# Linear attention with a gated MLP on one core: query and key features in groups of 128, 128, 128, 128, 64 rows, with the last group's low parts stacked under its high parts

## The chip, the cores and the metric

The kernel runs on one core of a Trainium2 chip. The metric is device time in microseconds (us), here of that one core. The engines are TensorE (PE; its weight loads are PEld), VectorE (DVE), ScalarE (ACT), GpSimd (POOL) and SyncE (SP, which issues most DMAs). Each works through its own queue in order; semaphores tie the queues together.

## What is computed

With x of 2048 tokens and 576 features, the kernel mixes two branches by a gate per token. The reference, cut to what matters:

```python
g = sigmoid((x * gate_w).sum(-1, keepdims=True))
# branch A, 32 heads of 18 features
q, k, v = split(x @ wqkv)
phi = lambda t: where(t > 0, t + 1, exp(t)) + 1e-6
pq, pk = phi(q), phi(k)
kv = einsum("bhsd,bhse->bhde", pk, v)          # per head
z = einsum("bhsd->bhd", pk)
num = einsum("bhqd,bhde->bhqe", pq, kv)
den = einsum("bhqd,bhd->bhq", pq, z)[..., None] + 1e-6
a = (num / den) @ wo
# branch B, Df = 4608
b = (gelu(x @ w_gate) * (x @ w_up)) @ w_down
return g * a + (1 - g) * b
```

## The kernel before

**Precision by parts.** Every fp32 operand is split into a rounded high part and a low part (the rest). ScalarE makes the high part, VectorE or GpSimd the low part (`split`, L67 to L69). A product is then three matmuls: high by high, high by low, low by high. They add up in the same PSUM bank.

**Stages.** (1) To about 119 us: key projections and, per 128 tokens, x^T times the key features (`grams`, L235), so that no value projection over tokens is needed. (2) To about 283 us: "mixing", the stage that the change edits. (3) The gate and up products of the MLP (L830), by a seven-product scheme, to about 1100 us, and (4) the down products (L1093) to the end. The first chain of stage 3 is interleaved with the end of stage 2.

**Heads in groups.** The 576 features of keys and queries lie in five groups of 7, 7, 7, 7 and 4 heads, that is 126, 126, 126, 126 and 72 rows (`GH`, `GR`, `GO`, L19 to L21). A group g fills one set of partitions.

**Mixing.** The order is written out by hand as a list of calls (L468 to L810, `tc.manual_schedule()`): what stands first in the text stands first in each engine's queue. Blocks b of 512 tokens come in the order 2, 3, 0, 1. The calls are:

- `query(b, g)` (L426): 14 matmuls of 512 tokens (L433) into one of three PSUM banks; then ScalarE's Relu (L435) and Exp (L436), and VectorE's L437, which gives r. L437 is the last reader of the bank.
- `states(kt)` (L445): kv per group from the grams and the value weights, ten matmuls for each of five kt (L452, L454); `key_sums_mm` (L462) the sums z.
- `states_out` (L523) and `key_sums` (L538) turn both into SBUF operands: kvt with a mask by heads, and zmk, whose columns pick the heads (L542, L543).
- `head_out(g)` (L546): a group's kv times its rows of wo (L553), split into KW[g]. `wo_load(g)` (L515) loads those rows and splits them (L519, L520); the loads stand in SP's queue.
- `halves_of(b, g)` (L561): r + eps as high part (ScalarE, L565) and low part (VectorE, L566), the tile hl, of which there are two. `den(b, g)` (L569): two matmuls (L575) that add the group's part to the denominators of all heads.
- `reciprocal(b, h)` (L640): denominators of 256 tokens to SBUF (L644, L645), reciprocal (L646), store to DRAM (L647). `reciprocals_load` (L649) reads them back (L651), each head's row repeated on its 18 partitions.
- `scaled(b, t)` (L670) for 128 tokens: r times the reciprocal (VectorE, L663), then the split into p, high part on ScalarE (L68) and low part on VectorE (L69).
- `mixed(b, t)` (L674): 5 groups x 3 parts x 2 column halves, 30 matmuls of 288 columns (L682) into one of two PSUM pairs; ScalarE scales the result by the gate (L687) and issues its store itself (L689).

Around the change the list interleaves these by hand: for example query(0,4) stands behind `reciprocals(3)` and ahead of scaled(2,2), and query(1,4) behind halves_of(1,0) and (1,1) and ahead of mixed(3,2). Token sums (L287 to L290 on VectorE, L621 on ScalarE) and loads for stage 3 are put between them. Behind query(1,4) ScalarE loads the table for Gelu (L772).

## Time and profile before

| | |
|---|---|
| time, median of 3 runs | 1504.03 us (1503.03 to 1504.7) |
| the profiled execution | 1503.88 us |
| its span, first to last instruction | 1502.1 us |
| mean granted TensorE clock | 1.000 |
| matmul queries, L433 | 280 matmuls, 14 for each of 20 (b, g) |
| matmul mixing, L682 | 480 matmuls, 30 for each of 16 (b, t) |
| matmul denominators, L575 | 40 matmuls |
| HBM read, written | 156.72 MB, 88.24 MB |

The page gives the busy time of each engine and its share of the span; matmuls are pipelined, so a busy PE is not PE at its peak, and the time from one matmul's start to the next tells more than the duration of one. The chain of waits goes back from the last instruction, at each step to what released it or to the one before it on its engine. A timeline row has its start, its duration (of a merged row, from the first start to the last end), the operation with out<-in, and in brackets how long the engine was idle before and for whom. All starts are in us from the span's start.

### The profile page before, as it was taken

How to read it: one execution, taken by the hardware profiler on the slowest of the kernel's cores; microseconds unless marked ns; L12 is line 12 of the kernel's file. 1: busy time of each engine (PE TensorE's matmuls, PEld its weight loads, DVE VectorE, ACT ScalarE, POOL GpSimd, SP SyncE). 2: the span in 40 equal slices, each digit the busy share in tenths (PEclk: the TensorE clock that was granted, in tenths of full speed). 3: DMA queues.
4: the chain of work that ended last, by engine and by line, in shares of the span. 5: the costliest groups of instructions: out<-in, count | busy, mean ns of one | idle time of the engine just before them, and what ended most of it. 6: DMA issues, size and time to landing. Idle time of an engine off the chain costs nothing.

```text
span 1502.1 us, 21595 instructions
## 1 busy us (share of the span) xinstructions
PE 1495.4 (100%) x8354; PEld 1320.4 (88%) x8354; DVE 1000.8 (67%) x1324; ACT 546.5 (36%) x711; POOL 716.6 (48%) x516
## 2 busy tenths in 40 slices
PE   9999999999999999999999999999999999999999
PEld 9998889878888888888888888888899999999999
DVE  7887776574666555666556665556677677777775
ACT  7554645333222233222232222332234454444431
POOL 1674533246554554654644644544347354553710
PEclk9999999999999999999999999999999999999999
DMA  7563464662333222332223332224777646565564
GB/s 250 166 205 118 165 249 166 240 248 91 141 140 115 96 106 105 140 141 97 100 102 123 141 122 103 99 98 167 292 285 265 213 153 216 169 213 187 198 201 136
DMA packets 98638, 246.36 MB, mean 164 GB/s; under 512 B 9056, under 2 KB 36344, under 8 KB 96104
## 3 DMA queue, kind: packets, MB, share of 16 engines
q1 hardware_dynamic: 95656, 235.42, 45.3%
q10 hardware_dynamic: 2880, 9.57, 1.8%
q8 instruction: 65, 1.06, 0.3%
q14 instruction: 37, 0.30, 0.1%
HBM read 156.72 MB, written 88.24 MB: 163 GB/s over the span
## 4 chain that ended last, share of the span: by engine, by line
PE 94%; DVE 3%; ACT 1%; issue 1%; DMA 1%; SPq 0%; ACTq 0%; DVEq 0%
PE bank L830 53%; PE bank L1093 27%; PE bank L433 4%; PE pair L682 3%; PE pair L244 2%; PE pair L199 2%; PE kpair L244 2%; PE kpair L199 2%; DMA raw<-wk 1%; DVE e L855 0%; PE den L575 0%; ACT p L68 0%; DVE r L663 0%; DVE hl L566 0%; PE pair L553 0%
## 5 line engine op out<-in xcount | busy, mean ns | idle before, releaser
L830 PE MATMUL bank<-xo,wg 128*128 128x512 f32 x1764 | 414.0, 395 | 1.3 <-DVE e L862 0.8
L830 PE MATMUL bank<-xo,wu 128*128 128x512 f32 (+1 forms) x1715 | 402.0, 395 | 0.1
L830 PEld LDWEIGHTS bank<-xo,wg 128*128 128x128 f32 x1764 | 332.2, 189 | 79.2 <-DVE e L862 1.2
L830 PEld LDWEIGHTS bank<-xo,wu 128*128 128x128 f32 (+1 forms) x1715 | 323.2, 189 | 75.8 <-ACT p L871 0.5
L1101 DVE SCALAR_TENSOR_TENSOR acc<-bank,gate,acc 128x288 f32<-128x288 f32 x288 | 140.7, 513 | 71.2 <-PE bank L1093 69.4
L283 POOL TENSOR_TENSOR stage<-stage 128x384 f32<-128x384 f32 x132 | 153.5, 1183 | 51.0 <-DMA stage<-wgu 48.4
L871 ACT ACTIVATE p<-bank 128x512 f32<-128x512 f32 x72 | 43.1, 599 | 332.4 <-PE bank L830 332.0
L844 POOL TENSOR_TENSOR wg<-stage,wg 128x768 fp32r<-128x768 f32 (+1 forms) x34 | 72.9, 2145 | 177.0 <-ACT wg L843 175.7
L844 POOL TENSOR_TENSOR wu<-stage,wu 128x768 fp32r<-128x768 f32 (+1 forms) x34 | 79.9, 2351 | 149.0 <-ACT wu L843 147.8
L1093 PE MATMUL bank<-wd,xo 128*128 128x288 f32 x1008 | 135.8, 294 | 0.0
L1093 PEld LDWEIGHTS bank<-wd,xo 128*128 128x128 f32 x1008 | 134.1, 188 | 0.0
L979 POOL TENSOR_TENSOR xo<-stage,xo 128x432 fp32r<-128x432 f32 x44 | 65.4, 1509 | 113.2 <-ACT xo L977 113.2
L876 DVE TENSOR_TENSOR u<-bank,p 128x512 f32<-128x512 f32 x72 | 49.5, 687 | 96.3 <-PE bank L830 86.8
L1093 PE MATMUL bank<-xo 128*128 128x288 f32 x792 | 107.1, 295 | 0.1
L1093 PEld LDWEIGHTS bank<-xo 128*128 128x128 f32 x792 | 105.7, 188 | 0.5 <-DVE u L865 0.4
L979 POOL TENSOR_TENSOR wd<-stage,wd 128x432 fp32r<-128x432 f32 x40 | 59.4, 1510 | 90.9 <-ACT wd L977 90.9
L862 DVE TENSOR_TENSOR e<-bank,u 128x512 f32<-128x512 f32 x54 | 37.2, 691 | 77.0 <-PE bank L830 76.9
L862 DVE TENSOR_TENSOR f<-bank,u 128x512 f32<-128x512 f32 x54 | 37.3, 692 | 71.6 <-PE bank L830 71.3
L852 ACT ACTIVATE f<-f 128x512 f32<-128x512 f32 x54 | 34.1, 633 | 132.8 <-DVE f L862 132.7
L984 POOL TENSOR_TENSOR stage<-stage 128x432 f32<-128x432 f32 x48 | 75.8, 1605 | 0.0
L890 DVE TENSOR_TENSOR u<-bank,u 128x512 f32<-128x512 f32 x72 | 49.8, 692 | 35.5 <-PE bank L830 33.3
L682 PEld LDWEIGHTS pair<-kw,p 126*128 126x128 f32 (+1 forms) x480 | 65.0, 188 | 2.0 <-DVE p L69 0.6
(192 smaller groups left out, 2310.0 us busy)
## 6 DMA issues: line engine op xcount, KB each, us to landing
h_d<-sx SPq DMA_DIRECT2D x108, 256.0 KB
stage<-wgu SPq DMA_DIRECT2D x34, 768.0 KB
xo<-h_d SPq DMA_DIRECT2D x29, 768.0 KB
e<-h_d SPq DMA_DIRECT2D x28, 768.0 KB
hraw<-h_d SPq DMA_DIRECT2D x27, 768.0 KB
h_d<-e SPq DMA_DIRECT2D x72, 256.0 KB
h_d<-f SPq DMA_DIRECT2D x72, 256.0 KB
stage<-wdn SPq DMA_DIRECT2D x6, 1728.0 KB
```

The source lines that it names most:

```text
L199: nc.tensor.matmul(out_t[:, :n], xa, kvw[i][:rows, r, lo:lo + n], start=(k == 0), stop=(k == 13))
L244: nc.tensor.matmul(y[:, n, :KH], a, p[:, n * KH:(n + 1) * KH], start=(k == 0), stop=(k == len(ops) - 1))
L283: nc.gpsimd.tensor_tensor(o, a, b, OP.subtract)
L433: nc.tensor.matmul(ps[:R], qw[i][:rows, rw, GO[g]:GO[g] + R], xa, start=(k == 0), stop=(k == 13))
L682: nc.tensor.matmul(y[:, i, :288], p[:R, a, g], KW[g][:R, wl, i * 288:(i + 1) * 288], start=(n == 0), stop=(n == 14))
L830: nc.tensor.matmul(ps, w_, x_, start=start and i == 0, stop=i == 6, skip_group_check=not start)
L844: nc.gpsimd.tensor_tensor(w[:, i, 3:5], src[:, :, 0:2], f32(w[:, i, 0:2]), OP.subtract)
L862: nc.vector.tensor_tensor(es[i], a, b, OP.add)
L979: nc.gpsimd.tensor_tensor(w[:, 1, c], src[:, c], f32(w[:, 0, c]), OP.subtract)
L984: nc.gpsimd.tensor_tensor(draw[:, o, c], draw[:, x, c], draw[:, y, c], OP.subtract)
L1093: nc.tensor.matmul(y, h[:, hl, g, t * 128:(t + 1) * 128], w[:, wl, g * 288:(g + 1) * 288], start=k in (1, 5) and n == 0, stop=n == len(ops ...
L1101: nc.vector.scalar_tensor_tensor(o, y, gate[:, 1, st:st + 1], o, op0=OP.mult, op1=OP.add)
```

## The change

Groups of query and key features now have 128, 128, 128, 128 and 64 rows: the 64 features that don't fit a fifth full group fill the two free partitions of each of the first four (`QORDER` gives the feature at each place). The value side and wo keep the old groups of 126 and 72 (`VR`, `VO`). What follows:

- **queries**: the fifth group's weights lie as 64 high columns and, right behind them, 64 low columns, so that one matmul of 128 columns gives both products with the high part of x. It has ten matmuls instead of 14. The lower products come out on partitions 64 to 127 and are added to the upper ones: a ScalarE copy, then a VectorE add within PSUM, both ahead of Relu.
- **halves_of, den**: for the fifth group the low part is written to partitions 64 to 127 of the same column block, and one matmul with a doubled zmk takes the place of two. `key_sums` makes zmk's second half with two more operations.
- **scaled_parts, mixed**: the fifth group's p has its low part under its high part, and KW[4] is repeated below itself (`rows_again`); two parts instead of three, 28 matmuls instead of 30. The low part is now made by two VectorE operations instead of one.
- **states**: two more small matmuls for each kt, for the key features that lie in other groups than their values.
- **head groups** in the order 4, 0, 1, 2, 3. `rows_out` copies the eight moved rows of KW[4] to the partitions 126 and 127 of KW[0] to KW[3] by four DMAs in SP's queue.
- **reciprocals**: 40 rows instead of 35; the read-back has a second DMA for the partitions 126 and 127.
- the query weights' low parts are made by two VectorE operations instead of one (`q_part`).

On VectorE, from the second block's reciprocals to the token sums, the queue reads before (L437 is the end of query(0,4), L663 and L69 are scaled(2,2)):

```order
L646 RECIPROCAL rb<-rb 35x256
L437 SCALAR_TENSOR_TENSOR r<-bank,r 72x512
L663 SCALAR_TENSOR_TENSOR r<-r,rb 126x5x128
L69 TENSOR_TENSOR p<-r,p 126x640
L287 TENSOR_TENSOR xc<-xc 128x512
```

and now:

```order
L690 RECIPROCAL rb<-rb 40x256
L459 TENSOR_TENSOR bank<-bank,r 64x512
L462 SCALAR_TENSOR_TENSOR r<-bank,r 64x512
L709 SCALAR_TENSOR_TENSOR r<-r,rb 128x5x128
L715 TENSOR_TENSOR p<-r,p 128x512
L716 TENSOR_TENSOR p<-r,p 64x128
L300 TENSOR_TENSOR xc<-xc 128x512
```

The add L459 stands between the reciprocal and the old next step, and the low part is two operations. On ScalarE the same place reads before (L644 reads the denominators, L435 and L436 are Relu and Exp of query(0,4), L68 the high part p(2,2)):

```order
L644 ACTIVATE rb<-den 35x256 x2
L435 ACTIVATE r<-bank 72x512
L436 ACTIVATE r<-r 72x512
L68 ACTIVATE p<-r 126x640
L687 ACTIVATE ga<-pair,gate 128x576
```

and now:

```order
L688 ACTIVATE rb<-den 40x256 x2
L458 ACTIVATE r<-bank 64x512
L460 ACTIVATE r<-bank 64x512
L461 ACTIVATE r<-r 64x512
L714 ACTIVATE p<-r 128x640
L734 ACTIVATE ga<-pair,gate 128x576
```

L458 is the copy that the add needs, and L460 is Relu, which needs the add. In SP's queue, the loads of wo's rows (raw<-wo) before:

```order
L302 DMA xsum_d_74<-xu 128x1024
L296 DMA xu<-xs 128x4x256
L517 DMA raw<-wo 128x576
L296 DMA xu<-xs 128x4x256
L517 DMA raw<-wo 128x576
L302 DMA xsum_d_75<-xu 128x1024
```

and now, with the four copies of KW rows:

```order
L315 DMA xsum_d_74<-xu 128x1024
L309 DMA xu<-xs 128x4x256
L593 DMA kw_1883<-kw_1887 2x1152
L593 DMA kw_1884<-kw_1887 2x1152
L593 DMA kw_1885<-kw_1887 2x1152
L593 DMA kw_1886<-kw_1887 2x1152
L549 DMA raw<-wo 128x576
L309 DMA xu<-xs 128x4x256
L549 DMA raw<-wo 128x576
```

Two loads of wo and what is behind them now follow four DMAs that read KW[4]. The diff, cut to its core:

```diff
-GH = [7, 7, 7, 7, 4]
-GR = [n * DH for n in GH]
-GO = [126 * g for g in range(5)]
+VR, VO = [126, 126, 126, 126, 72], [126 * g for g in range(5)]
+QR, QO = [128, 128, 128, 128, 64], [128 * g for g in range(5)]
+QORDER = [d for g in range(4) for d in (*range(126 * g, 126 * g + 126), 568 + 2 * g, 569 + 2 * g)] + [*range(504, 568)]
...
+    def q_part(w, kt, raw):
...
+            nc.scalar.activation(w[:, h:h + D], raw, AF.Copy)
+            nc.vector.tensor_tensor(w[:, l:l + 512], raw[:, :512], f32(w[:, h:h + 512]), OP.subtract)
+            nc.vector.tensor_tensor(w[:, h + D:h + 640], raw[:, 512:], f32(w[:, h + 512:h + D]), OP.subtract)
...
     def query(b, g):
-        R = GR[g]
+        R = QR[g]
...
+        for k, (wa, xa) in enumerate(ops):
+            nc.tensor.matmul(ps[:wa.shape[1]], wa, xa, start=(k == 0), stop=(k == len(ops) - 1), skip_group_check=g == 4)
+        if g == 4:
+            nc.scalar.activation(r, ps[64:], AF.Copy)
+            nc.vector.tensor_tensor(ps[:R], ps[:R], r, OP.add)
         nc.scalar.activation(r, ps[:R], AF.Relu, scale=-1.0)
...
     def states(kt):
...
+            parts = [(o[:, :, :n], o[:, 0, :n], gm[:, :, c])]
+            if g == 4:
+                more = gm[:, :, :512].rearrange("p a (g c) -> p a g c", g=4)[:, :, :, 126:]
+                into = o[:, :, 64:].rearrange("p a (g c) -> p a g c", g=4)
+                parts.append((into, into[:, 0], more))
...
     def states_out():
...
+        split(kvt[:72, 0, 4, :72], kvt[:72, 1, 4, :72], kvm[:72, 4, :72])
         split(kvt[:126, 0, :4], kvt[:126, 1, :4], kvm[:126, :4])
-        split(kvt[:72, 0, 4, :72], kvt[:72, 1, 4, :72], kvm[:72, 4, :72])
...
     def key_sums():
...
+            for rows in (slice(0, R),) if g < 4 else (slice(0, 64), slice(64, 128)):
+                nc.vector.tensor_scalar(zmk[rows, g, :64], sg, z, None, op0=OP.mult)
+                nc.vector.scalar_tensor_tensor(zmk[rows, g, 64:], sg, z, f32(zmk[:R, g, :64]),
+                                               op0=OP.mult, op1=OP.subtract)
...
+    def rows_out():
+        for g in range(4):
+            nc.sync.dma_start(f32(KW[g][126:]), f32(KW[4][64 + 2 * g:66 + 2 * g]))
+
+    def rows_again():
+        nc.scalar.activation(KW[4][64:, 0], f32(KW[4][:64, 0]), AF.Copy)
...
     def halves_of(b, g):
...
+        lo = hl[:, 1] if g < 4 else hl[64:, 0]
         nc.scalar.activation(hl[:R, 0], r, AF.Copy, bias=EPS)
-        nc.vector.scalar_tensor_tensor(hl[:R, 1], r, EPS, f32(hl[:R, 0]), op0=OP.add, op1=OP.subtract)
+        nc.vector.scalar_tensor_tensor(lo, r, EPS, f32(hl[:R, 0]), op0=OP.add, op1=OP.subtract)
...
-        for a in range(2):
-            nc.tensor.matmul(den_of[b], zmk[:GR[g], g], hl[:GR[g], a], start=(g == 0 and a == 0),
-                             stop=(g == NG - 1 and a == 1), skip_group_check=True)
+        for a in range(2 if g < 4 else 1):
+            nc.tensor.matmul(den_of[b], zmk[:, g], hl[:, a], start=(g == 0 and a == 0),
+                             stop=g == NG - 1, skip_group_check=True)
...
+    WO = (4, 0, 1, 2, 3)
...
-        head_out(g)
+        head_out(WO[g])
+        if g == 1:
+            rows_out()
         if g + 2 < NG:
-            wo_load(g + 2)
+            wo_load(WO[g + 2])
...
+        for k, (rows, heads, times) in enumerate(((slice(0, 126), 7, DH), (slice(126, 128), 1, 2))):
+            nc.sync.dma_start(rb_of[b, h][rows], bass.AP(
...
     def scaled_parts(b, t):
...
-        split(p[:126, 0], p[:126, 1], r)
+        nc.scalar.activation(p[:, 0], r, AF.Copy)
+        nc.vector.tensor_tensor(p[:, 1, :4], r[:, :4], f32(p[:, 0, :4]), OP.subtract)
+        nc.vector.tensor_tensor(p[64:, 0, 4], r[:64, 4], f32(p[:64, 0, 4]), OP.subtract)
...
-            for a, wl in ((0, 0), (0, 1), (1, 0)):
+            for a, wl, R in ((0, 0, 128), (0, 1, QR[g]), (1, 0, 128))[:3 if g < 4 else 2]:
...
     halves_of(3, 1)
+    rows_again()
```

More of the change, by code (lines that the diff above doesn't have):

```diff
@@ L47, in tile_gated_mix @@
     probe = keep.tile([128, 8], F32, name="probe")
-    rden_d = {(b, h): dram.tile([7 * NG, BS // 2], F32, name=f"rden_d{b}{h}") for b in range(NB) for h in range(2)}
+    rden_d = {(b, h): dram.tile([HROWS * NG, BS // 2], F32, name=f"rden_d{b}{h}") for b in range(NB) for h in range(2)}
     xop_d = dram.tile([128, 3, 5, BS], F32, name="xop_d")
@@ L100, in tile_gated_mix @@
     x8 = qwp.tile([128, 5, BS], F32R, name="x8")
-    qw = [qwp.tile([128, 5, D], F32R, name=f"qw{i}") for i in range(2)]
+    qw = [qwp.tile([128, 5 * D], F32R, name=f"qw{i}") for i in range(2)]
+    Q_HI, Q_LO = (0, 640, 1280), (1856, 2368)
     aheads = Scope()
@@ L268, in load @@
             nc.sync.dma_start(raw[:, :D], wq[i, kt])
-            todo.append(lambda: w_part(qw[i], kt, raw, 0, D))
+            todo.append(lambda: q_part(qw[i], kt, raw[:, :D]))
         else:
```

86 lines of the change are left out of this document (50 added, 36 removed).

## The prediction

> **What bounds the kernel now.** I read the page first, then the busy time by stretch, then the chain of waits in order of time, then each engine's timeline from 119 to 311 us, the only stretch in which edited instructions matter. The page:
>
> ```profile
> span 1502.1 us, 21595 instructions
> PE 1495.4 (100%) x8354; PEld 1320.4 (88%) x8354; DVE 1000.8 (67%) x1324; ACT 546.5 (36%) x711; POOL 716.6 (48%) x516
> ```
>
> TensorE is busy all the time, so the first reading is that every matmul taken out is time won. The stretches (length, then PE, PEld, DVE, ACT, POOL busy, clock, DMA share, GB/s) say that this holds in the mixing part too:
>
> ```profile
> 119.30:191.15 71.85, 71.85 (x395) 60.85 (x394) 49.60 (x80) 38.35 (x69) 29.98 (x26) 1.00 0.42 150
> 191.15:243.35 52.20, 52.14 (x316) 46.03 (x314) 37.47 (x47) 29.03 (x44) 19.58 (x20) 1.00 0.57 205
> 243.35:283.00 39.65, 39.58 (x270) 37.79 (x271) 19.75 (x25) 15.28 (x21) 6.82 (x4) 1.00 0.73 254
> ```
>
> The chain of waits (start, us, engine, tile, line) tells more:
>
> ```profile
> 171.30 0.46 PE den L575 x2
> ...
> 191.15 3.25 PE bank L433 x14
> 194.40 4.00 PE pair L682 x30
> ...
> 209.62 0.73 ACT ga L687
> ...
> 235.27 0.49 ACT r L435
> ...
> 236.44 0.53 ACT L772
> ...
> 242.47 0.84 DVE p L69
> 243.35 3.71 PE pair L682 x26
> ...
> 310.02 786.47 PE bank L830 x3381
> ```
>
> From 209.62 to 243.35 no piece of the chain is TensorE's: ScalarE and VectorE hand work to each other in program order without a pause, and at 243.35 mixed(0,0) waits for the low part p. The timeline of VectorE shows that this tight run starts earlier, right behind mixed(2,0), which ends at 191.15:
>
> ```profile
> 192.76 0.41 DVE L645 TENSOR_TENSOR rb<-rb,den 35x256 f32<-35x256 f32 x1 [1.80 <-ACT rb L644]
> ...
> 195.27 1.75 DVE L646 RECIPROCAL rb<-rb 35x256 f32<-35x256 f32 x1
> 196.94 0.62 DVE L437 SCALAR_TENSOR_TENSOR r<-bank,r 72x512 f32<-72x512 f32 x1
> ...
> 199.09 0.83 DVE L69 TENSOR_TENSOR p<-r,p 126x640 fp32r<-126x640 f32 x1 [0.81 <-ACT p L68]
> 199.84 0.95 DVE L287 TENSOR_TENSOR xc<-xc 128x512 f32<-128x512 f32 x1
> ```
>
> Followed from 191.15 (copy out of mixed(2,0), two reciprocals, query(0,4), scale(2,2), and so on), no step up to 243.35 waits for TensorE. So this stretch has two bounds of the same length, 52.2 us of matmuls and 52.2 us of ScalarE and VectorE in turn. The change shortens the first and lengthens the second. From 310.02 on TensorE alone counts, and nothing there is edited.
>
> **The change: TensorE's own work.** A query matmul takes 3.25/14 = 0.232 us, a denominator 0.46/2 = 0.23, one of mixing 4.00/30 = 0.133. Removed: 4 x 4 query matmuls 3.71, 4 denominators 0.92, 16 x 2 of mixing 4.27, together 8.9. Added: two narrow state matmuls for each of five kt. The nearest rows are the last group's pair and what follows it:
>
> ```profile
> 144.75 0.24 PE L452 MATMUL bank<-gt,wv 128*72 128x144 f32 x1
> 144.83 0.20 PE L454 MATMUL bank<-gt,wv 128*72 128x72 f32 x1
> 144.87 1.14 PE L465 MATMUL bank<-ones,rs 128*126 128x2 f32 x10
> ```
>
> Two starts in 0.12 us: 0.06 each; the ten of one stationary load with 2 columns take about 0.1 each, so 0.6 to 1.0 for ten, of which I take 0.6, the row with the same 72 weight columns. The net is -8.3 us. Whether it is kept is decided stretch by stretch.
>
> **Up to 119 us.** The query weights' low parts become two pieces (four more VectorE operations), in a part where TensorE leads, and the last one is read only behind the others: 0.
>
> **119 to 191 us.** query(b,4) gets a ScalarE copy of the upper half and a VectorE add, and Relu and Exp now stand behind that add; ScalarE takes nothing else meanwhile. The rows around query(2,4), ScalarE, VectorE and TensorE:
>
> ```profile
> 150.30 0.58 ACT L435 ACTIVATE r<-bank 72x512 f32<-72x512 f32 x1
> 150.91 0.63 ACT L436 ACTIVATE r<-r 72x512 f32<-72x512 f32 x1
> ```
> ```profile
> 152.96 0.24 DVE L542 TENSOR_SCALAR zmk<-cs,zc 72x64 fp32r<-72x64 f32 x1
> ...
> 153.44 0.68 DVE L437 SCALAR_TENSOR_TENSOR r<-bank,r 72x512 f32<-72x512 f32 x1
> ...
> 177.62 0.62 DVE L566 SCALAR_TENSOR_TENSOR hl<-r,hl 126x512 fp32r<-126x512 f32 x1
> ```
> ```profile
> 156.39 0.63 PE L575 MATMUL den<-hl,zmk 126*128 126x512 f32 x2
> ...
> 178.08 1.07 PE L575 MATMUL den<-hl,zmk 126*128 126x512 f32 x4
> ```
>
> Today Relu and Exp of query(2,4) are done while VectorE still makes zmk. Now the add stands behind a sixth pair of zmk operations (153.44 - 152.96 = 0.48) and states that end about 0.48 later: at 154.40. Add 0.68, Relu 0.58, Exp 0.63 and three or four hand-overs of 0.03 to 0.04: L437 at 156.42, the low part hl(2,0) done at 157.7. TensorE gets to den(2,0) at 156.39 + 0.60 - 0.93 = 156.06 and to its second matmul at 156.3: a wait of 1.45. Likewise hl(3,1) stands on VectorE behind query(3,4), four KW low parts and two reciprocals: 178.24 done today, about 1.3 later now (copy 0.58, add 0.68), against den(3,1) at about 178.75: a wait of 0.8. mixed(2,0) waits some 0.25 more for p(2,0). Sum: +0.6, two queries -1.86, two denominators -0.46, one tile -0.27, waits +2.5: **+0.5** when mixed(2,0) ends. Reversing the order of the head groups costs nothing itself: the same loads, copies and matmuls in another order.
>
> SP's queue: its four copies of KW rows wait for KW[4], and two loads of wo that are issued at about 143 today stand behind them.
>
> ```profile
> 143.61 0.57 SPq L517 DMA_DIRECT2D raw<-wo  x1
> ...
> 253.54 0.27 SPq L647 DMA_DIRECT2D rden_d<-rb  x1
> 255.00 0.76 SPq L651 DMA_DIRECT2D rb<-rden_d  x1
> ...
> 277.08 0.33 SPq L834 DMA_DIRECT2D stage<-wgu  x1
> ```
> ```profile
> 283.22 4.07 POOL L283 TENSOR_TENSOR stage<-stage 128x384 f32<-128x384 f32 x4 [23.50 <-DMA stage<-wgu]
> ```
>
> KW[4] is split at about 161 (behind L437 at 156.42 ScalarE has two hl copies, four Relu and Exp of 0.6 and the split itself); four issues of some 0.35 and the load's own make 163. A small write is back 1.2 us after its issue (253.81 to 255.00), 768 KB take 5.8 (277.41 to 283.22), so these 288 KB land between 164 and 169. ScalarE's copy of them holds hl(2,3) and the next Relu, but query(3,4) ends at about 169.4 (today 171.30 less two head groups of 6 x 0.133 and a denominator, 169.2, and 0.2 by the sum so far), and by then ScalarE has caught up: 0. The KW rows themselves are needed 20 us later, and ScalarE's copy of KW[4] for the stack, some 0.7, lies below the reciprocals. The eight read-backs of two rows cost SP some 0.3 each; only the last is waited for, at 271.50 (below).
>
> **191 to 243 us, the ScalarE and VectorE run.** (1) query(0,4): its matmuls end below the reciprocals and Relu and Exp are hidden there; L437 follows the second reciprocal at 196.94. Now the add comes there, then Relu and Exp, then L437: 0.68 + 0.58 + 0.63 + 0.12 = +2.0. Behind the waiting Relu on ScalarE stand p(2,2), for which mixed(2,2) waits, and hl(0,0), for which den(0,0) waits. (2) The low part p takes 199.84 - 199.09 = 0.75 of VectorE. It becomes 128x512 and 64x128 written at partition 64. Bounds come from rows of such narrow pieces:
>
> ```profile
> 120.39 0.22 DVE L231 TENSOR_TENSOR xg<-xn,xg 128x64 fp32r<-128x64 f32 x1
> 120.64 0.75 DVE L151 TENSOR_TENSOR qw<-raw,qw 32x576 fp32r<-32x576 f32 x1
> 121.42 0.76 DVE L250 TENSOR_TENSOR g_sum<-pair,g_sum 128x576 f32<-128x576 f32 x1
> ```
>
> VectorE mostly starts the next operation 0.08 before the last is done (199.09 + 0.83 against 199.84), but on both sides of the one that writes at partition 64 nothing overlaps (120.61 to 120.64, 121.39 to 121.42). With overlap the two pieces take 0.86, without 0.97. Three of them are on the run, (2,2), (3,0), (3,1): +0.33 to +0.66; hl(0,4), which now writes at partition 64, adds 0.2 in the second case; I take the second, since the row is the same kind of write. The Trainium skill, "VectorE: DVE Perf Modes", section "Two Vector instructions with no wait between them", says that an instruction whose input or output starts in another 32-partition group than the one before is held until all earlier ones finish. By that rule, which the rows at 120.64 and 121.42 bear out, the stretch gains 5.0, without it 4.3, and the forecast would be 1507.4. (3) query(1,4):
>
> ```profile
> 235.01 1.28 DVE L566 SCALAR_TENSOR_TENSOR hl<-r,hl 126x512 fp32r<-126x512 f32 x2
> ```
>
> ScalarE starts its Relu at 235.27 and the table load at 236.44. Now the add waits for both hl (235.01 + 1.28 + 0.22), then Relu and Exp: the table load at 236.5 + 0.68 + 0.58 + 0.63 + 0.1 = 238.5: +2.1. Behind it stand hl(1,2), hl(1,3) and p(0,0), the ones that den(1,2), den(1,3) and mixed(0,0) need. Together 2.0 + 0.66 + 0.2 + 2.1: **+5.0**. TensorE saves 4.0 here (two queries 1.86, seven tiles 1.87, a denominator 0.23) and waits it all away, some 9 us idle in sum.
>
> **243 to 283 us.** p(0,0) comes 0.5 + 5.0 = 5.5 late. TensorE then takes back 0.23 and eight tiles x 0.27 = 2.4, but not all:
>
> ```profile
> 254.40 0.74 ACT L687 ACTIVATE ga<-pair,gate 128x576 f32<-128x576 f32 x1 [1.63 <-DMA ga_d<-ga]
> ```
> ```profile
> 271.50 0.82 DVE L663 SCALAR_TENSOR_TENSOR r<-r,rb 126x640 f32<-126x640 f32 x1 [2.01 <-DMA rb<-rden_d]
> ```
>
> ScalarE's copy at 254.40 waits for a store that it issued itself behind its big weight load, so p(0,3) behind it comes 5.5 late too, and so does the reciprocals' read-back at 271.50, ahead of p(1,2). TensorE comes to mixed(0,3) some 4.2 late, after a quarter of its saving, and to mixed(1,2) 4.4 late; with today's margins of some 0.5 and 1 there I estimate waits of 0.8 and 0.2: **-1.4** net. What follows to 310.02 starts from the last tile and moves as a whole.
>
> Sum: +0.5 + 5.0 - 1.4 = +4.1 on the profiled execution's 1503.88 (span 1502.1 and 1.8 around it), which lies 0.15 below the median of 1504.03: **1508.0 us**.
>
> **The rivals.** *TensorE's count decides, faster:* VectorE is busy for 37.47 of 52.20 us and ScalarE for 29.03, so each has gaps, and the new operations might fall into them. It decides if the run has 8 us of slack; then -8.3: 1495.6. Against it: the gaps are hand-overs in one dependent run, with no wait for TensorE. *Half is hidden, the same:* the run meets TensorE at places that I count as tight, GpSimd slows VectorE less at the new times (0.95 at 199.84 for 512 columns, against 0.76 for 576 at 121.42), and half of the 5.0 is absorbed, while TensorE keeps more of its own: 0.5 + 2.5 - 2.0 = +1.0: 1504.9. *The load behind the KW rows, slower still:* the first wo load behind them lands after 169.4 and ScalarE, with query(3,4)'s copy, stands still from there, microsecond for microsecond. At 172 it is +2.6 on top: 1510.6. Against it: even 5.8 us from issue to landing is in time.
>
> **How the numbers follow.** Forecast 0.50 (own range 1505.4 to 1510.4, +1.5 to +6.5, for each of the four waits may be off by half a microsecond and the run by one or two), TensorE's count 0.15, half hidden 0.25, the load 0.10. A measurement of this kernel tells 0.2%, 3 us, from no change. Slower: four fifths of the forecast and the load, 0.5. Same: the rest of the forecast and most of the half-hidden case, 0.3. Faster: 0.2. The range of 8 in 10 leaves out the full gain below and little above: 1499 to 1511.
>
> **What would show it.** TensorE idle of several us between 191 and 250 where there is 0.06 now, with den(0,b), mixed(2,2) and mixed(0,0) waiting for hl and p; the VectorE operation behind the reciprocals at 196.94 followed by a ScalarE Relu before L462; mixed(0,0) about 5 us later than 243.35; the down part as long as before. It is wrong if TensorE stays full from 191 to 243 and mixed(0,0) comes earlier than now.

## The result and the profile after

The changed kernel takes 1515.31 us (median of 6 runs, 1514.34 to 1516.78), beside 1503.76 us (1503.03 to 1504.70) for the kernel before: a ratio of 1.0078, 95% interval 1.0065 to 1.0091. It is slower, as forecast, but by about 11 us where 4 were forecast, and outside the range.

The page of the changed kernel and its busy time by stretch (length, then PE, PEld, DVE, ACT and POOL busy, clock, DMA share, GB/s):

```profile
span 1513.1 us, 21566 instructions
```
```profile
119.30:191.15 71.85, 68.33 (x361) 56.75 (x359) 48.59 (x80) 38.13 (x69) 30.94 (x26) 0.98 0.38 132
191.15:243.35 52.20, 50.40 (x282) 41.93 (x282) 38.22 (x53) 26.28 (x41) 19.68 (x20) 1.00 0.56 202
243.35:283.00 39.65, 37.49 (x218) 32.59 (x219) 24.80 (x36) 18.15 (x27) 7.03 (x4) 0.96 0.57 206
```

TensorE, which before was idle for 0.06 us from 191 to 243, now has gaps in all three stretches, and in two of them the clock is below 1.00. The forecast had 2.5 us of waits in the first stretch, but in other places: of the 3.52 us there, 2.43 stand at head_out(3) (rows below), where it had none. The clock was not in the forecast. The gaps of the second do not show all that was lost there, since the same window now holds fewer matmuls.

A better measure is how long each stage takes. The stages are cut at starts in TensorE's timeline: query(2,4), query(0,2), mixed(0,0), the gate product behind the last tile, and the first product that waits for VectorE's e (310.02 before). In us, each a difference of two starts of one trace; the experiments are explained below:

| kernel | (2,4) to (0,2) | to mixed(0,0) | to the gate product | to e |
|---|---|---|---|---|
| before | 33.12 | 63.57 | 39.51 | 27.95 |
| after | 37.50 | 68.74 | 41.35 | 27.15 |
| KW rows later | 33.67 | 68.94 | 41.51 | 27.36 |
| full rows in mixing | 37.35 | 68.33 | 39.28 | 28.01 |
| query group 4 plain | 33.52 | 65.29 | 40.22 | 27.63 |
| only (2,4) plain | 33.62 | 68.62 | 41.31 | 27.16 |
| the three edits | 32.85 | 65.07 | 39.33 | 28.62 |
| before, 64 rows | 33.12 | 66.70 | 42.17 | 27.18 |
| the three edits, fourth order | 32.85 | 62.96 | 38.21 | 27.33 |
| before, fourth order | 33.12 | 63.40 | 39.14 | 27.25 |

After against before: +4.38, +5.17, +1.84 and -0.80. Only the second comes near the forecast. query(2,4) itself starts at 145.89 in the one and 145.87 in the other, and the gate and up products behind the last cut are as long as before (786.27 against 786.47), all that follows to the end nearly so (1192.47 against 1192.08).

The first 4.38. The chain of waits of the changed kernel, from VectorE's add of query(2,4) on:

```profile
153.99 0.62 DVE bank L459
154.63 0.60 ACT r L460
...
159.95 0.67 DVE kw L70
160.67 0.76 SPq L593
...
163.41 0.40 SPq L549
163.91 0.63 SPq L309
164.58 6.37 DMA raw<-wo
171.03 0.74 issue
171.80 1.40 POOL wos L552
```

This is the queue in which the forecast put 0. The four copies of KW rows (L593) wait for KW[4], the two wo loads (L549) stand behind them, and the second of the two needs 6.37 us from its issue at 164.58. ScalarE and GpSimd then split it for head_out(3). TensorE's timeline at that place:

```profile
171.78 0.53 PE L586 MATMUL pair<-wos,kvt 126*126 126x288 f32 x2 [1.48 <-ACT wos L551]
173.25 0.79 PE L586 MATMUL pair<-wos,kvt 126*126 126x288 f32 x4 [0.95 <-POOL wos L552]
173.88 0.55 PE L616 MATMUL den<-hl,zmk 128*128 128x512 f32 x1
174.23 8.09 PE L456 MATMUL bank<-xo,qw 128*128 128x512 f32 x28
182.16 1.40 PE L616 MATMUL den<-hl,zmk 128*128 128x512 f32 x4
```

TensorE waits 1.48 for ScalarE's high part and 0.95 for GpSimd's low part. After that, the 28 matmuls of query(0,0) and query(0,1) take 182.16 - 174.23 = 7.93 us instead of 28 x 0.232 = 6.50, at a lower clock (below).

The 5.17 up to mixed(0,0) is the run of ScalarE and VectorE, and its rows on VectorE are as forecast: behind the second reciprocal comes the add, then a wait for ScalarE's Relu and Exp, then L462, then the low part as two operations:

```profile
199.83 1.75 DVE L690 RECIPROCAL rb<-rb 40x256 f32<-40x256 f32 x1
201.50 0.67 DVE L459 TENSOR_TENSOR bank<-bank,r 64x512 f32<-64x512 f32 x1
203.49 0.68 DVE L462 SCALAR_TENSOR_TENSOR r<-bank,r 64x512 f32<-64x512 f32 x1 [1.32 <-ACT r L461]
...
205.71 0.69 DVE L715 TENSOR_TENSOR p<-r,p 128x512 fp32r<-128x512 f32 x1 [0.80 <-ACT p L714]
206.43 0.29 DVE L716 TENSOR_TENSOR p<-r,p 64x128 fp32r<-64x128 f32 x1
206.75 0.69 DVE L300 TENSOR_TENSOR xc<-xc 128x512 f32<-128x512 f32 x1
```

The 1.84 behind it was forecast as a gain of 1.4. The tiles do not get shorter: 28 matmuls of mixed(2,1) stand from 198.04 to 202.05 in TensorE's timeline, 4.01 us, as long as 30 before (194.24 to 198.23). TensorE's weight loads of that tile say why:

```profile
197.81 3.61 PEld L729 LDWEIGHTS pair<-kw,p 128*128 128x128 f32 x26
201.59 0.29 PEld L729 LDWEIGHTS pair<-kw,p 64*128 64x128 f32 x2 [0.17 <-issue]
202.04 0.99 PEld L456 LDWEIGHTS bank<-x,qw 128*128 128x128 f32 x5 [0.16 <-issue]
```

The stacked group's second product has only 64 rows (p with the low part of KW[4]). Ahead of its weight load TensorE stands for 0.17 us, and ahead of the next one with 128 rows for 0.16. And mixed(0,0) itself takes 5.67 us, from its start to that of the denominator behind it, at a lower clock in this execution (last section). TensorE's timeline at both tiles:

```profile
198.04 4.08 PE L729 MATMUL pair<-kw,p 128*128 128x288 f32 x28
202.05 1.89 PE L456 MATMUL bank<-x,qw 128*128 128x512 f32 x7
...
252.13 5.74 PE L729 MATMUL pair<-kw,p 128*128 128x288 f32 x28 [1.01 <-ACT p L714]
257.80 0.50 PE L616 MATMUL den<-hl,zmk 128*128 128x512 f32 x1
```

### The profile page after: what moved, and what is told of

Read it like the earlier page. It is cut to its first block, busy times and chain, and to the rows that moved or that the text cites. A ratio compares the mean times of both kernels' runs of the same rounds, so it can differ in the third digit from the quotient of the medians.

```text
span 1513.1 us, 21566 instructions
## 1 busy us (share of the span) xinstructions
PE 1500.1 (99%) x8312; PEld 1318.2 (87%) x8312; DVE 1013.6 (67%) x1350; ACT 549.2 (36%) x716; POOL 717.9 (47%) x516
## 4 chain that ended last, share of the span: by engine, by line
PE 89%; DVE 3%; DMA 2%; ACT 2%; issue 1%; POOL 1%; SPq 1%; ACTq 0%; DVEq 0%; POOLq 0%
PE bank L878 53%; PE bank L1141 24%; PE pair L729 2%; PE pair L257 2%; PE pair L212 2%; PE kpair L212 2%; PE kpair L257 2%; PE bank L456 1%; DMA xsum_d<-xu 1%; DMA stage<-wdn 0%; DMA xo<-h_d 0%; DVE hl L607 0%; DMA xu<-wgu 0%; POOL wd L1027 0%; DMA raw<-wo 0%
## 5 line engine op out<-in xcount | busy, mean ns | idle before, releaser
L729 PE MATMUL pair<-kw,p 128*128 128x288 f32 x448 | 67.8, 306 | 1.4 <-ACT p L714 1.4
```

Source lines behind the costliest of these rows:

```text
L729: nc.tensor.matmul(y[:, i, :288], p[:R, a, g], KW[g][:R, wl, i * 288:(i + 1) * 288], start=(n == 0), stop=(n == 13))
```

## Experiments: where the 11 us come from

My theory now had four costs: (A) the late fifth wo load, with the slower matmuls behind it, about 3.9; (B) the longer run of ScalarE and VectorE, 5.0; (C) the two switches per tile to 64 rows and back, 16 x 0.28 = 4.5; (D) the clock in mixed(0,0), 1.5. The rival: the longer run of ScalarE and VectorE is all of the loss, and the rest only fills time that TensorE would have waited anyway. They overlap (A and B in part have one source, as will be seen), so they need not add up to 11, and (D) has no run of its own. Each kernel was run 5 or 11 times beside the kernel before.

**KW rows later.** Their four DMAs are given to SP behind the head groups' loop, so that no wo load stands behind them.

```diff
-        if g == 1:
-            rows_out()
...
+    rows_out()
     ahead_load(5)
```

> The changed kernel with the KW rows' loads given to SP's queue behind the output weights' loads (ahead_load(5)) instead of between query groups 0 and 1. Theory of four costs (the late fifth wo load with the colder clock behind it, about 3.9 us; the longer run of ScalarE and VectorE between mixed(2,0) and mixed(0,0), 5.0; the switches to 64 rows in mixing, 16 times 0.28; the clock's drop in mixed(0,0), 1.5): the waits of 1.48 and 0.95 us in head_out(3) go, the 28 matmuls of query(0,0) and query(0,1) take 6.5 us again instead of 7.9, query(0,2) begins about 4 us earlier, and the total is 1511 (1510 to 1513). Rival (the longer run of ScalarE and VectorE is all of the loss, and the late load only takes up time that TensorE would have waited anyway): query(0,0) begins earlier, but query(0,4) is waited for as late as now, and the total falls by less than 1 us, 1514.5 to 1515.5.

Measured: 1511.4 us (1510.54 to 1512.94), ratio 1.0052 (1.0039 to 1.0066), 3.9 under the changed kernel. TensorE's timeline has no wait at head_out(3), and the 28 matmuls take 6.46:

```profile
171.00 0.96 PE L586 MATMUL pair<-wos,kvt 126*126 126x288 f32 x6
...
172.03 6.62 PE L456 MATMUL bank<-xo,qw 128*128 128x512 f32 x28
178.49 0.86 PE L616 MATMUL den<-hl,zmk 128*128 128x512 f32 x3
```

The first stage falls from 37.50 to 33.67, the others stay. (A) holds with its size, and the rival, under 1 us, is out.

**Full rows in mixing.** The second product of group 4 runs over 128 rows; the low parts' lower 64 rows of KW[4] are zeros, so nothing else changes.

```diff
+        nc.scalar.activation(KW[4][64:, 1], f32(KW[4][:64, 1]), AF.Copy, scale=0.0)
...
-            for a, wl, R in ((0, 0, 128), (0, 1, QR[g]), (1, 0, 128))[:3 if g < 4 else 2]:
+            for a, wl, R in ((0, 0, 128), (0, 1, 128), (1, 0, 128))[:3 if g < 4 else 2]:
```

> The changed kernel with the second product of group 4 in mixing over all 128 rows; the added 64 rows of the low parts of KW are zeros, so the result is the same and the count of matmuls too. Theory of four costs: the 0.17 us ahead of the 64-row weight load and the 0.16 us behind it go, the 28 matmuls of a tile take 3.73 us instead of 4.00, and of 16 tiles the eight or so behind mixed(0,0) shorten the total by 2 to 2.5 us, all sixteen at most by 4.5: 1511 to 1513.3. Rival (TensorE waits for ScalarE and VectorE everywhere, so its own count is of no account): a tile's matmuls are shorter but its successor waits as much longer, 1514.5 to 1515.5.

Measured: 1514.23 us (1513.9 to 1514.51), ratio 1.0070 (1.0058 to 1.0083): 1.1 less, under the 2 to 2.5 of the theory and over the rival's nothing. The gaps in the weight loads are gone, and the tile takes 3.72 (198.03 to 201.75):

```profile
198.03 3.64 PEld L730 LDWEIGHTS pair<-kw,p 128*128 128x128 f32 x27
201.62 1.47 PEld L456 LDWEIGHTS bank<-x,qw 128*128 128x128 f32 x7
```

From query(0,4) to mixed(0,0) it takes 56.52, in the changed kernel 56.51: the 7 x 0.28 saved there are waited away to the last tenth, as the forecast said of TensorE's savings in that stretch. From mixed(0,0) to the gate product 2.07 are won (41.35 to 39.28), and 0.86 is given back on the way to e (27.15 to 28.01). Of the 2.07, 1.37 lie in mixed(0,0) alone (5.67 to 4.30), for the most part the clock's, which held in this execution; the switches' own share is some 0.7 to 1.0. So (C) is right as a mechanism, but counts only behind mixed(0,0), and for less than the theory had.

**Query group 4 plain.** 14 matmuls of 64 columns, no copy, no add; mixing and denominators stay stacked, the KW rows stay where the change has them.

```diff
-                ops += [(w[:, hi:hi + 128], x[:, kt]), (w[:, hi:hi + R], x[:, 3 + kt])]
-                if g < 4:
-                    ops.append((w[:, lo:lo + 128], x[:, kt]))
+                lo = lo if g < 4 else hi + 64
+                ops += [(w[:, hi:hi + R], x[:, kt]), (w[:, hi:hi + R], x[:, 3 + kt]), (w[:, lo:lo + R], x[:, kt])]
...
-        if g == 4:
-            nc.scalar.activation(r, ps[64:], AF.Copy)
-            nc.vector.tensor_tensor(ps[:R], ps[:R], r, OP.add)
```

> The changed kernel with query features of group 4 made without stacking: 14 matmuls of 64 columns into one sum, and neither ScalarE's copy of the lower half nor VectorE's add behind it; mixing and denominators stay stacked. Theory of four costs: of the 5.0 us that the run of ScalarE and VectorE between mixed(2,0) and mixed(0,0) grew by, the 4.1 for query(0,4) and query(1,4) go and 4 matmuls (0.93 us) come back there, so the total falls by 3 to 4, with less waiting at 249 to 252 us possibly by 1.5 more: 1510 to 1512. Rival (that run is all of the loss): the total falls by 8 to 10, to 1505 to 1507.

Measured: 1506.3 us (1505.66 to 1507.52), ratio 1.0018 (1.0009 to 1.0026): 9.0 less, where the theory had 3 to 5.5 and the rival 8 to 10. But the rival's number came by a road that it did not name. The run to mixed(0,0) gives 3.45 (68.74 to 65.29), in the 3 to 4 that (B) said, though the theory took four matmuls back where two queries have eight: by its own sum it would have been 2.2, so the added matmuls must in part fill time in which TensorE had waited. Behind mixed(0,0) 1.13 more go, where the clock holds (that tile takes 4.30 again, 64 rows and all). The first stage gives as much again, 3.98, the very 3.9 of the late load, though SP's order is unchanged. So the costs are not four separate ones: the stacked query also makes the load late.

**The three edits together.**

> The changed kernel with all three edits: KW rows loaded later, full 128 rows in mixing, query group 4 not stacked. What is left of the change then: mixing and denominators with the low parts stacked. Theory of four costs: the three gains add, 4 + 2.3 + 4, to 1503 to 1506, about the kernel before. Rival (one cause only): no more than the single best of the three edits, within 1 us.

Measured: 1505.35 us (1504.66 to 1506.34), ratio 1.0011 (1.0003 to 1.0020): the number is in the theory's span, the sum is not. One by one the edits gave 3.9 + 1.1 + 9.0 = 14.0, together 10.0, since the plain query has the late load in it already.

**Only (2,4) plain.** This tests the link: the copy, the add and ScalarE's wait for it are taken away for query(2,4) alone.

```diff
+        stacked = g == 4 and b != 2
...
-        if g == 4:
+        if stacked:
             nc.scalar.activation(r, ps[64:], AF.Copy)
             nc.vector.tensor_tensor(ps[:R], ps[:R], r, OP.add)
```

> The changed kernel with query(2,4) alone made without stacking, the other three as they are, and the KW rows' loads where the change has them. Theory of the linked wait (ScalarE's 3.60 us wait for the add of query(2,4), which stands on VectorE behind the key sums, makes head_out(0)'s split late by 2.1, with it the KW rows on SP's queue and the wo load behind them): the fifth wo load lands about 2 us earlier, head_out(3) waits at most 0.3, and the total falls by 3 to 4.5, to 1511 to 1512.3, although SP's order is unchanged. Rival (the place behind the four KW rows alone makes the load late): the waits in head_out(3) stay near 2 and the total falls by less than 1.

Measured: 1512.11 us (1511.08 to 1513.03), ratio 1.0058 (1.0044 to 1.0071): 3.2 less, as the link said. ScalarE's timeline in the changed kernel (Relu behind the add, and the split of head_out(0)):

```profile
154.63 0.59 ACT L460 ACTIVATE r<-bank 64x512 f32<-64x512 f32 x1 [3.60 <-DVE bank L459]
...
159.13 0.63 ACT L69 ACTIVATE kw<-pair 72x576 fp32r<-72x576 f32 x1
```

and with (2,4) plain (L463 is Relu), then SP's queue of the same kernel:

```profile
150.61 0.58 ACT L463 ACTIVATE r<-bank 64x512 f32<-64x512 f32 x1
...
157.27 0.63 ACT L69 ACTIVATE kw<-pair 72x576 fp32r<-72x576 f32 x1
```
```profile
158.82 2.68 SPq L596 DMA_DIRECT2D kw<-kw  x4
161.54 0.40 SPq L552 DMA_DIRECT2D raw<-wo  x1
...
162.72 0.61 SPq L552 DMA_DIRECT2D raw<-wo  x1
```

In the changed kernel Relu waits 3.60 us, because the add stands on VectorE behind twelve key-sum operations. The split is 1.86 later than here, the KW rows too (160.67 against 158.82), the last wo load too (164.58 against 162.72). Two conditions must meet: the load behind the KW rows, and a ScalarE that is late by some 2 us. Undoing either is enough: the first stage is 33.67 with the one, 33.62 with the other, and with both (the three edits) 32.85.

**Before, 64 rows.** The switch by itself, in the kernel without any stacking: one product of the last group over 64 of 72 rows, eight rows of it left out.

```diff
+                K = 64 if g == 4 and wl else R
...
-                    nc.tensor.matmul(y[:, i, :288], p[:R, a, g], KW[g][:R, wl, i * 288:(i + 1) * 288],
+                    nc.tensor.matmul(y[:, i, :288], p[:K, a, g], KW[g][:K, wl, i * 288:(i + 1) * 288],
```

> The kernel before with one product of the last group in mixing (high parts of p with low parts of KW) over 64 of its 72 rows; eight rows of that product are left out. Nothing else moves, the count of matmuls included. Theory of the switch (two weight loads each wait 0.16 to 0.17 us where the rows go from over 64 to 64 and back): the 30 matmuls of a tile take 4.3 us instead of 3.99, 16 tiles 4.5 us, and since TensorE has almost no waits there the total rises by 3 to 4.7, to 1506.5 to 1508.2. Rival (the gap belongs to the changed kernel's stacked tile or its rows 64 to 127, not to the 64 rows): 1503.2 to 1503.9.

Measured: 1508.72 us (1508.56 to 1509.19), ratio 1.0033 (1.0021 to 1.0046). Less work, 5.1 us more. The weight loads of one tile:

```profile
194.40 3.61 PEld L683 LDWEIGHTS pair<-kw,p 126*128 126x128 f32 x26
198.17 0.29 PEld L683 LDWEIGHTS pair<-kw,p 64*128 64x128 f32 x2 [0.16 <-issue]
198.63 0.30 PEld L683 LDWEIGHTS pair<-kw,p 72*128 72x128 f32 x2 [0.16 <-issue]
```

The 26 loads of the first row are 24 of 126 rows and two of 72, without a gap between them. A gap of 0.16 stands ahead of the 64 rows, and another ahead of the 72 that follow them. The tile takes 4.38 (194.63 to 199.01 in TensorE's timeline) instead of 3.99, more than the 4.3 expected and than the 0.28 in the stacked tile; what the last 0.1 is, these rows do not say. The switch is the cause, not the stacking. The Trainium skill, "TensorEngine Tiling (Array Packing)", section "Key Properties", says that a change of the tiling mode drains TensorE, and lists 64 rows and 128 rows as different modes under "Available Configurations". The trace agrees with such a drain, at 0.16 to 0.17 us each, and the row count alone brings it on here. That the chip changes its mode at these loads is a reading that no run shows directly.

## Experiments: can the saved matmuls reach the end?

With the three edits TensorE has 16 x 0.27 (a tile of 3.72 for 3.99) and 4 denominators of 0.23 less to do than the kernel before, and the total is still not under it. The rest stands in waits for ScalarE and VectorE, so I tried other orders of the same steps. The first moves query(0,4) ahead of mixed(2,0), halves(1,0) and (1,1) ahead of the reciprocals of 0, scaled(0,0) ahead of halves(1,2), and the Gelu table load back.

```diff
+    query(0, 4)
     mixed(2, 0)
     reciprocals(3)
-    query(0, 4)
...
+    halves_of(1, 0)
+    halves_of(1, 1)
     reciprocals(0)
     mixed(3, 1)
     scaled(3, 3)
-    halves_of(1, 0)
-    halves_of(1, 1)
```

> All three edits (later KW rows, full rows in mixing, query group 4 not stacked) and four steps in another order: query(0,4) ahead of mixed(2,0), halves(1,0) and (1,1) ahead of the reciprocals of 0, scaled(0,0) ahead of halves(1,2) and (1,3), and the Gelu table's load behind halves(1,4). Theory (what is left of TensorE's savings stands in waits for ScalarE and VectorE: 0.88 at mixed(2,0), 0.72 at den(1,1), 0.80 at mixed(0,0)): these go, the total falls by 1.5 to 2.5 against the three edits alone, to 1503 to 1504, level with the kernel before. Rival (the start of the MLP, which waits for its weights and for Gelu, takes back whatever comes earlier): 1505 to 1505.5, as without the new order.

Measured: 1511.76 us, ratio 1.0053 (1.0040 to 1.0065): 6.4 slower than without the new order, which neither side expected. VectorE's timeline:

```profile
246.91 0.83 DVE L705 SCALAR_TENSOR_TENSOR r<-r,rb 128x640 f32<-128x640 f32 x1 [3.92 <-DMA rb<-rden_d]
```

scale(0,0) needs the reciprocals after their trip out and back by DMA, and I had put more work ahead of the reciprocals and scale(0,0) ahead of the work that covered the trip. den(1,2), now behind it, waits 3.72, and mixed(0,0) takes 5.78 us (251.75 to 257.53) at a lower clock, where the three edits alone had 4.30.

The next one only moves the reciprocals of 3 and query(0,4) ahead of mixed(2,0), and halves(0,0) and (0,1) ahead of the token sums.

```diff
-    mixed(2, 0)
     reciprocals(3)
     query(0, 4)
+    mixed(2, 0)
...
-    token_sums(0, 0)
     mixed(2, 1)
     halves_of(0, 0)
     halves_of(0, 1)
+    token_sums(0, 0)
```

> The three edits (later KW rows, full rows in mixing, query group 4 not stacked) with two steps in another order: the reciprocals of 3 and query(0,4) ahead of mixed(2,0), and halves(0,0) and (0,1) ahead of VectorE's token sums. Theory (ScalarE and VectorE's order sets when query sums, halves and p come, and TensorE's savings stand in the waits for them): the 0.88 us at mixed(2,0) goes and the 0.71 at den(0,3) shrinks, the total falls by 1 to 1.5 against the three edits alone, to 1504 to 1504.4. Rival (behind 283 us the MLP's start waits for its own weights and takes back what comes earlier): 1505 to 1505.5.

Measured: 1504.29 us (1503.17 to 1505.3), ratio 1.0001 (0.9992 to 1.0010): level with the kernel before, 1.1 under the three edits. The same with the reciprocals of 0 earlier, and the token sums of 1 behind them:

```diff
-    token_sums(1, 0)
     query(1, 2)
...
+    den(0, 4)
     scaled(3, 2)
+    reciprocals(0)
+    token_sums(1, 0)
     token_sums(1, 1)
     query(1, 3)
-    den(0, 4)
-    reciprocals(0)
```

> As the one with the reciprocals of 3 first, and also halves(0,4), den(0,4) and the reciprocals of 0 ahead of the token sums and of query(1,3), so that the chain from den(0,4) over VectorE's reciprocals and the round trip by DMA to scale(0,0) starts some 3 us earlier. Theory: the waits of 0.72 at den(1,1) and 0.80 at mixed(0,0) shrink too, the total falls by 2 to 3 against the three edits alone, to 1502.4 to 1503.4, level with the kernel before or just under it. Rival (the MLP's start takes it back): within 0.4 of the run beside it.

Measured: 1507.34 us, ratio 1.0025 (1.0016 to 1.0034), a miss: ScalarE's copy of a token chunk now stands for 6.18 us in front of query(1,3)'s Relu, waiting for sums behind two reciprocals.

```profile
231.55 1.92 ACT L661 ACTIVATE xo<-xc 128x2048 fp32r<-128x2048 f32 x1 [6.18 <-DVE xc L303]
```

A second order moves the token sums of 1 further back, and their copy behind scaled(0,0):

```diff
     halves_of(1, 1)
+    token_sums(1, 0)
     query(1, 4)
...
     scaled(0, 0)
+    token_sums(1, 1)
```

> The three edits (later KW rows, full rows in mixing, query group 4 not stacked), the reciprocals of 3 and query(0,4) ahead of mixed(2,0), halves(0,0) and (0,1) ahead of the token sums, den(0,4) and the reciprocals of 0 ahead of query(1,3); the token sums of 1 come behind halves(1,1), their copy by ScalarE behind scaled(0,0), the Gelu table behind halves(1,4). The run with the reciprocals of 0 early failed because ScalarE stood 6.18 us for those sums; that is gone here. Theory: the waits left between mixed(2,0) and mixed(0,0) are under 1 us, and the total is 1502 to 1503.2, 0.5 to 1.7 under the kernel before. Rival (the MLP's start takes back what comes earlier): 1504 to 1504.5, as with the reciprocals of 3 first.

Measured: 1505.23 us, ratio 1.0010 (1.0001 to 1.0019), another miss. GpSimd's low parts of the chunk start at 242.68 for 5.54 us, and VectorE beside them needs 1.39, 1.26 and 1.78 for what takes 0.69, 0.29 and 0.68 elsewhere; den(1,4) waits 3.40. GpSimd's timeline, then VectorE's:

```profile
242.68 5.54 POOL L664 TENSOR_TENSOR xo<-xc,xo 128x512 fp32r<-128x512 f32 x4 [28.29 <-ACT xo L661]
```
```profile
244.40 1.39 DVE L711 TENSOR_TENSOR p<-r,p 128x512 fp32r<-128x512 f32 x1 [1.71 <-ACT p L710]
245.80 1.26 DVE L712 TENSOR_TENSOR p<-r,p 64x128 fp32r<-64x128 f32 x1
246.99 1.78 DVE L604 SCALAR_TENSOR_TENSOR hl<-r,hl 64x512 fp32r<-64x512 f32 x1
```

The kernel before in the same second order:

> The kernel before with the same new order and nothing else. Theory (TensorE has almost no waits there, so there is nothing for an order to free): 1503 to 1504.2. Rival (the order itself is what gains, whatever the stacking): as much under the kernel before as the run beside it, 1502 to 1503.2.

Measured: 1506.35 us, ratio 1.0018 (1.0010 to 1.0027): 2.7 slower, where 0 was expected. The order gains nothing by itself; here too a denominator waits, den(1,4) for 1.48. A third order with the copy and GpSimd's part behind scaled(0,2):

```diff
     mixed(0, 0)
     den(1, 4)
     scaled(0, 2)
+    token_sums(1, 1)
     reciprocal(1, 0)
     reciprocals_load(1, 0)
+    token_sums(2, 0)
     token_sums(2, 1)
```

> As the second order, with ScalarE's copy and GpSimd's low parts of the token chunk 1 moved behind scaled(0,2), and the token sums of 2 behind the first reciprocal of 1. In the second order GpSimd's 5.54 us stood beside VectorE's low parts and halves(1,4), which took 1.39, 1.26 and 1.78 us instead of 0.69, 0.28 and 0.68, and den(1,4) waited 3.40. Theory: that wait goes, mixed(0,1) follows mixed(0,0) at once, the total is 1502 to 1503.2, 0.5 to 1.7 under the kernel before. Rival (GpSimd's work now stands beside the MLP's start, whose products wait for these low parts, and takes it back): 1504 to 1506.

Measured: 1509.09 us, ratio 1.0037 (1.0023 to 1.0051), worse again: GpSimd's work beside the next sums on VectorE makes ScalarE wait 7.88 us for them, and mixed(0,3) waits 6.62 for the p behind.

The fourth order starts from the reciprocals of 3 first and leaves the copy of chunk 1 ahead of the reciprocals of 0, so that GpSimd runs beside them; in the rows of the runs above reciprocals take 1.75 us wherever they stand.

```diff
-    token_sums(1, 0)
     query(1, 2)
     den(0, 2)
     halves_of(0, 4)
+    token_sums(1, 0)
     den(0, 3)
     mixed(3, 0)
+    den(0, 4)
     scaled(3, 2)
     token_sums(1, 1)
-    query(1, 3)
-    den(0, 4)
     reciprocals(0)
+    query(1, 3)
...
-    nc.scalar.activation(probe, probe, AF.Gelu_apprx_tanh)
...
     halves_of(1, 4)
+    nc.scalar.activation(probe, probe, AF.Gelu_apprx_tanh)
```

> The run with the reciprocals of 3 first, and besides: halves(0,4) ahead of the token sums of 1, den(0,4) straight behind mixed(3,0), the copy of chunk 1 by ScalarE ahead of the reciprocals of 0 and these ahead of query(1,3), so that GpSimd's low parts stand beside the reciprocals again; the Gelu table behind halves(1,4). Theory (TensorE's saved time reaches the end once the waits for ScalarE and VectorE are gone): the waits of 0.73 at den(1,1) and 0.71 at mixed(0,0) go, the total falls by 0.8 to 1.8 against the run with the reciprocals of 3 first, to 1502.5 to 1503.5. Rival (the MLP's start is set by its weights and Gelu, and no order of what stands ahead of it brings the saving through): mixed(0,0) begins earlier, the total stays at 1504 to 1504.6.

Measured: 1502.58 us (1500.85 to 1504.1) beside 1504.09 for the kernel before, ratio 0.9991 (0.9982 to 1.0000). In the profiled execution the stages from query(2,4) to e sum to 161.35 us, 2.80 less than before, and the stage with the MLP's start (27.33) takes back none of it. Its busy times by stretch:

```profile
191.15:243.35 52.20, 50.92 (x314) 45.36 (x313) 38.99 (x54) 27.72 (x42) 18.92 (x20) 1.00 0.59 213
243.35:283.00 39.65, 39.07 (x257) 36.14 (x256) 22.57 (x32) 16.83 (x24) 8.55 (x6) 1.00 0.69 254
```

The kernel before in that order:

> The kernel before with the order that, with the three edits and stacked mixing and denominators, came out 1.5 us under it, and nothing else. Theory (the gain is TensorE's saved matmuls, let through by the order): TensorE has nothing to save here, its stretch from 191 to 283 us stays full, and the total is 1503 to 1505. Rival (the order gains by itself): 1501.5 to 1502.9.

Measured: 1502.92 us (1502.42 to 1503.54) beside 1503.47, ratio 0.9996 (0.9987 to 1.0005). That is between the two accounts: the median lies at the border of what they were to give. From query(2,4) to e the trace of this run sums to 162.91 (the kernel before had 164.15), so 1.24 of the 2.80 come with the order alone, and 1.56 are left for TensorE's fewer matmuls. But the stacked kernel's profiled execution, 1501.06, is the second fastest of its eleven, the medians of the two kernels differ by 0.34, and their ranges overlap. So the best version stands level with the kernel before in the same order; whether it is 1 us better is not shown.

## Why the prediction was wrong

The direction was right and the sum was not: +4.1 forecast, +11.0 in the spans.

- **The states, +0.6: right.** From the first query product to query(2,4) it takes 27.01 (118.88 to 145.89), before 26.39.
- **"ScalarE caught up: 0", SP's queue: failed**, and cost 3.8 to 3.9. Most of its working held: KW[4]'s split at 159.95 to 160.6 for "about 161", the issues done at 163.4 for 163. The failed step is the landing: "between 164 and 169" was worked out for a load issued at 163, but only the first of the two is issued then (163.41), and the one that TensorE waits for is issued at 164.58 behind a load of xs, and takes 6.37 where I had taken 5.8 as an upper bound. The rival "the load behind the KW rows" described this mechanism, and I gave it 0.10 and 2.6 us on top; it was also more: 2.43 of waits at head_out(3) and 1.43 in the 28 matmuls behind it. That 1.43 is the clock's here; where the clock held, VectorE was late by about as much instead (1.30 at den(3,1), last section).
- **The wait at den(2,0), 1.45: its mechanism right.** Waits of 0.76 and 0.30 stand there, and L462 starts at 155.92 for the forecast 156.42. The 0.8 at den(3,1) does not show behind the late load, but without it (KW rows later) 0.72 stands there.
- **The run of ScalarE and VectorE, +5.0: right.** From query(0,4) to mixed(0,0) it is 56.51 (195.62 to 252.13), before 51.57 (190.99 to 242.56), so +4.94. The parts hold too: without stacked queries 3.72 of it goes (191.97 to 244.76 is 52.79, eight more matmuls included). The low part's two operations take 1.04 from L715's start to L300's, for the forecast 0.97. The rival that half of the run is hidden is out with it.
- **"TensorE then takes back 0.23 and eight tiles x 0.27": failed.** The step counted a tile as matmuls times 0.133 and did not ask whether the one of 64 rows costs more than the others. It costs 0.28 more per tile, so a tile stays at 4.01. With the clock in mixed(0,0) this turned -1.4 into +1.84. The waits behind it were too small as well: with full rows and the clock at 1.00 the stage is 39.28, only 0.23 under the kernel before, so of the 2.4 that TensorE then does save, about 2.2 go into waiting, where the forecast had 1.0 (0.8 and 0.2).
- **TensorE's count decides (0.15): out**, and more so than argued: of the 8.3 us on paper 4.5 were no saving on TensorE either, since the switches took them.

Sum in the trace up to e: -0.6 at the start, +5.2 to query(0,4) where 0.5 were forecast, +4.94 where 5.0 were, +1.84 for -1.4, and -0.80 behind it for 0: 10.6.

## What to carry to other kernels

Count what each matmul's shape costs, not only how many there are: here a product of 64 rows in the middle of full ones cost as much (0.28 to 0.39 us a tile) as the two matmuls saved, one of 72 rows cost nothing extra, and filling the 64 up to 128 with zeros cost TensorE nothing. When a step is given one more hand-over between two engines, follow everything that stands behind the waiting instruction on its engine, through the DMA queues, to the last load and not to the first; two delays that cost little alone met in one load here. A saving on one engine of a tight hand-over run is worth nothing until the order lets it through, and most orders tried made a new wait instead.

## What the runs showed of the hardware that I had not expected

The cost of a change of row count on TensorE, 0.16 to 0.17 us, is above. The other is the clock. In the changed kernel the granted clock (the column ahead of the DMA share) falls after waits far shorter than the stretch that then runs slowly:

```profile
174.00:176.00 2.00, 2.00 (x7) 1.51 (x6) 0.68 (x2) 1.58 (x3) 1.80 (x3) 0.51 1.10 343
176.00:178.00 2.00, 2.00 (x7) 1.60 (x6) 2.00 (x4) 1.61 (x4) 1.88 (x3) 0.64 0.99 411
...
252.00:254.00 2.00, 1.87 (x9) 1.80 (x10) 1.80 (x3) 0.71 (x2) 0.00 (x0) 0.63 0.86 233
254.00:256.00 2.00, 2.00 (x10) 2.00 (x10) 1.21 (x3) 1.26 (x2) 0.00 (x0) 0.51 1.03 403
```

In the profiled execution with full rows in mixing, nearly the same waits leave it alone:

```profile
174.00:176.00 2.00, 2.00 (x12) 1.71 (x12) 0.83 (x2) 1.10 (x2) 1.84 (x3) 1.00 1.01 313
...
254.00:256.00 2.00, 2.00 (x17) 2.00 (x17) 1.18 (x4) 1.26 (x2) 0.00 (x0) 1.00 0.96 394
```

The waits ahead of 174 sum to 2.43 us there (1.48 and 0.95) and to 2.26 here (1.31 and 0.95). The Trainium skill, "TensorE: Matmul & The Clock Gate", section "What's actually happening", says that the clock halves after an idle window of about 3.4 us and that the window runs freely, so that the point varies. The trace agrees that it varies; it shows the drop after less idle time, spread over several waits with a few matmuls between them. What decides was not tested, but the 64 rows are not needed for it: mixing, the only place that has them, begins at 191 in both kernels, behind the first drop, and mixed(0,0) with full rows slowed down too in the first new order (5.78 us). Nor is it fixed by the kernel: the mean clocks of the changed kernel's six executions are 0.997, 1.000, 1.000, 0.997, 0.997 and 0.999, those of the five with full rows 1.000, 0.997, 0.999, 0.999 and 1.000. So these slow stretches belong to the executions that were profiled. The changed kernel's two executions at 1.000 took 1514.42 and 1514.34 us, still 10.6 over the kernel before: the clock is a small part of the loss. The drop ahead of 174 cost little by itself: where the clock held, den(3,1) waited 1.30 for VectorE instead, and query(0,2) began at the same place (37.35 against 37.50).
